# Column sums in four column strips, later q and k loads without a wait for V, and the first layer's first groups ahead of a unit's products with V

## The chip, the cores and the metric

The kernel runs on one core of one Trainium2 chip. The metric is the device time of one execution in microseconds (us), lower is better. Before the change it is 308.14 us, the median of three runs (307.33 to 308.79). The traces come from the hardware profiler and show one execution each.

## What is computed

Attention in a sliding window over 8 sequences of 576 tokens with 8 heads of 64, and then a two-layer block on the 4608 rows of 512 that come out of it:

```python
scores = scale * np.matmul(q, k.transpose(0, 1, 3, 2))
mask = np.abs(pos[:, None] - pos[None, :]) <= window      # window = 32
scores = np.where(mask, scores, -1000000000.0)
attn = np.exp(scores - np.max(scores, axis=-1, keepdims=True))
attn = attn / (np.sum(attn, axis=-1, keepdims=True) + 1e-09)
x = np.matmul(attn, v)                                    # as (4608, 512)
...
h = x @ w_in                                              # 512 x 2048
r = np.maximum(h, 0.0)
g = s * (r * r) + b
out = g @ w_out                                           # 2048 x 512
```

Since `g @ w_out` is `s * (r*r) @ w_out + b * (column sums of w_out)`, the kernel adds a row of column sums of w_out, times b, to each output row. That row is called CVEC.

## The kernel before

**Who sets the order.** Every operation is a task of one of five streams (TensorE "pe", ScalarE "act", VectorE "dve", GpSimd "pool", and "sp", which issues the DMAs), with what it reads and writes, a cost and a key. A planner (`_Graph.plan`) runs the tasks through a model of the engines and takes, again and again, the task that can start first; the key decides between tasks that could start at the same time. The result is one fixed order for each engine. Each engine then works through its order strictly, and a task that waits holds up all that stands behind it on its engine. All loads and stores, and the DMA transposes, go through the one queue of SP.

**Attention.** The tokens are worked in units of 128 (`unit`, `finish`): the scores of a unit (`qk_part`), exp on ScalarE, a mask on VectorE, the products with V (`av_part`, line 839), a reciprocal and a scaling on VectorE, and a transposition into XT, the input of the first layer. The V of a unit is loaded as f32 (line 589) and cast to bf16 into VB (lines 597 and 598); EV0, EV1 and EV2 name the engine of that cast for the first, the second and the later sequences. Units are counted through: sequence 0 has units 0 to 4 and so on; from sequence 3 on (LONG = 3) all tokens are one long row with units 0 to 22 in the trace's order, of which the last sequence begins at unit 18.

**q and k.** For the first three sequences they are cast, turned by TensorE (lines 628, 660, 673) and copied to SBUF. From sequence 3 on (`later`, `piece`) they are loaded in three pieces (lines 707 and 714: q, k, and the last 64 tokens of both), cast on ScalarE or POOL (line 733) and turned by DMA transposes (line 749). A piece waits for an earlier unit's products (`paced`), and, before the change, for the load of the last V unit of the sequence before it. Units from number 25 on are also turned into XT by DMA transposes (line 887).

**The first layer.** Blocks of 512 tokens; the first three blocks are cut smaller (SPLIT: block 0 into 224, 128 and 160 tokens, blocks 1 and 2 into two times 256). `s1` computes some columns of 128 of the hidden layer: matmuls on TensorE into one of two banks W (line 1097), ReLU on ScalarE (line 1104), the square on VectorE (line 1110). FIRST lists the order in which the first pieces (token piece, quarter of the 2048 columns) are made. W_in and W_out come in 8 loads each (line 561) and are cast by POOL (line 564).

**The second layer.** `second` makes each block of 512 tokens in seven products instead of eight (line 1154), with sums and differences of the hidden layer (line 1146) and of W_out (line 1126, `weight_sums`, partly in place in W_out). VectorE combines products into the output rows (line 1170), SP stores them (line 1179).

**The first minute of a run.** `first_units` makes the products with V of sequence 0: unit 2 and later wait for the transposition of the unit two before. `constant` makes CVEC: 16 matmuls with a weight matrix of ones add up the rows of W_out over 16 chunks of 128 rows, in one bank (line 1228), and VectorE multiplies by b (line 1231). Because the weights are all ones and 128 wide, each of the 128 output rows gets the same sums.

Of the kernel before, what the change touches and what calls it, by code (L numbers as in the profile page):

```python
# [5 lines left out]
F32 = mybir.dt.float32  # L6
# [3 lines left out]
ALU = mybir.AluOpType  # L10
# [11 lines left out]
PAIRS = 3  # L22
# [7 lines left out]
ORDER2 = ("t", "q0", "k0", "v0", "q1", "k1", "v1", "v2", "v3", "v4")  # L30
WINE = ("pool", "pool", "pool", "pool")
SPLIT = {0: (224, 128, 160), 1: (256, 256), 2: (256, 256)}
FIRST = ((0, 0), (1, 0), (0, 1), (2, 0), (1, 1), (2, 1), (0, 2), (1, 2), (2, 2), (0, 3), (1, 3), (2, 3))
WOUTE = (("pool", "pool"),) * 4
SWITCH = 215.0
XTS = 4000.0
# [4 lines left out]
PACE = ((-1, -1, -1),) * 3  # L41
CASTS = 40.0
LATE = 8
# [2 lines left out]
SLACK = (1000.0, 2000.0, 3000.0, 3000.0)  # L46
PACEV = ((-1,-1,0,0,1),(0,0,1,1,2),(0,0,1,1,2))
EARLY = -22.0
EV0 = ("dve", "act", "pool", "dve", "pool")
BANK1 = ("O", "AVN", "SC", "O", "AVN")  # L50
EV1 = ("pool", "pool", "pool", "pool", "pool")
EV2 = ("dve",) * 5
# [270 lines left out]
def bass_sliding_window_symmetric__then__act_starrelu_kernel(  # L323
# [23 lines left out]
    with ExitStack() as es:  # L347
        uid = {"n": 0}

        def seq_of(b):  # L350
            return min(b, LONG)
# [7 lines left out]
        def sb(shape, dt, nm):  # L359
            uid["n"] += 1  # L360
            return es.enter_context(nc.sbuf_tensor(f"{nm}_{uid['n']}", list(shape), dt))
# [39 lines left out]
        TW = [sb((128, 8, HN), BF16, "tw") for _ in range(3)]  # L401
        GSUM = sb((128, 8, HT), BF16, "gsum")
        CVEC = sb((128, DM), F32, "cvec")
        SB128 = sb((128, 2), F32, "sb128")
        SROW = sb((128, 2), F32, "srow")

# [14 lines left out]
        add = g.add  # L421
# [34 lines left out]
        def group_of(b):  # L456

            if b < LONG:
                return range(NUNIT)
            u0 = (NTILE * (b - LONG)) // 2  # L460
            return range(u0, (NTILE * (b + 1 - LONG) + (b == B - 1)) // 2)
# [106 lines left out]
        def paced(b, u):  # L568

            c, v = seq_of(b - 1), group_of(b - 1)[0] + u  # L570
            while v < 0:
                c, v = c - 1, v + NUNIT
            return land["av", c, v]
# [180 lines left out]
        def later(b, key):  # L754
            slot = b % 2
            if b < PAIRS + 2:
                for c0, x in ((0, 0), (160, WIN + S)):
                    add("pool", lambda e, c0=c0: e.memset(QTS[slot][:, :, c0:c0 + 16], 0.0), 400,
                        writes=[("QTZ", slot, x)] + [(t, slot, x, pr) for t in ("QT", "KT") for x in range(NTILE) for pr in range(NPAIR)],
                        key=key - 20.0)  # L760
            for i, parts in enumerate(((("q", 0, 512, 0),), (("k", 0, 512, 0),), (("q", 512, 64, 0), ("k", 512, 64, 64)))):
                piece(b, parts, key + 0.01 * i, [paced(b, PACE[min(b, 4) - 2][i])] +
                      ([land["v", seq_of(b - 1), group_of(b - 1)[-1]]] if b > PAIRS or LATE == PAIRS else []))

# [125 lines left out]
        def pe_part(key, av=None, sc=None, waits=()):  # L892

            parts = [p for p in (av, sc) if p]
            fns, mark = list(sc[0]) if sc else [], None
            if av:
                mark = len(av[0][0]) - 1
                fns = av[0][0] + fns + [None] + av[0][1]
            t = add("pe", fns, SWITCH + sum(p[3] for p in parts) + (0.0 if sc else 20.0),
                    reads=[r for p in parts for r in p[1]], writes=[r for p in parts for r in p[2]], key=key,  # L900
                    slack=1500.0 if key < due(2, 0) - 1 else SLACK[2], waits=waits)
            t.mark = mark
            return t
# [58 lines left out]
        def first_units():  # L962
            for u in range(NUNIT):
                bank, res = av_banks(0, u)
                stir(("av", u), res[0], bank[:, 0, :], -25.0 + u)
                land["av", 0, u] = pe_part(-25.0 + u, av=av_part(0, u), waits=[land["xt", u - 2]] if u > 1 else [])
                finish(0, u, -25.0 + u)

        last, closed = [], [0]
# [25 lines left out]
        def attention():  # L995
            seq = {"k": -200.0}

            def nxt():
                seq["k"] += 1.0
                return seq["k"]  # L1000

            def weights(step):
                which, i, x = {"w": "in", "o": "out"}[step[0]], int(step[1]), "ab".index(step[2])
                load_weights(which, i, x, nxt(), WINE[i] if which == "in" else WOUTE[i][x])

            for pr in range(NPAIR):
                for name in "qk":
                    load_pair(name, pr, nxt())
                    turn_pair(name, pr, -60.0 + 0.1 * pr, banks, K0[pr] if name == "k" else Q0[pr], 200.0)
                pair_scores(0, pr)  # L1010
            for t in ORDER0:
                if t == "t":
                    part(0, "t", nxt(), -23.5, banks, 200.0)
                    late_scores()
                elif t[0] == "v":
                    u = int(t[1])
                    load_v(0, u, nxt(), "sp")
                    cast_v(0, u, -28.0 + u, EV0[u], 300.0)
                else:
                    weights(t)  # L1020
            first_units()
            for step in ORDER1:
                if step == "s":
                    yield S
                elif step == "c":
                    for i, src in enumerate((moe_s, moe_b)):
                        add("sp", lambda e, i=i, src=src: e.dma_start(SROW[0:128:32, i:i + 1], src.partition_broadcast(4)),
                            600.0, writes=[("SROW", i)], dma=("l", 1, 15.0), key=nxt())
                    add("dve", lambda e: e.stream_shuffle(SB128[:, :], SROW[:, :], [0] * 32), 150,
                        reads=[("SROW", 0), ("SROW", 1)], writes=[("SB128", 0), ("SB128", 1)], key=P2[0, 0] - 8.0, slack=500.0)  # L1030
                elif step[0] in "wo":
                    weights(step)
                elif step[0] == "v":
                    load_v(1, int(step[1]), nxt(), "sp")
                    cast_v(1, int(step[1]), EARLY + 1.0 + 0.1 * int(step[1]), EV1[int(step[1])], 800.0)
                else:
                    part(1, step, nxt(), EARLY + 0.1 * FOURS.index(step), banks1, 500.0)
                    if step[0] == "k":
                        for pr in (2 * int(step[1]), 2 * int(step[1]) + 1):
                            pair_scores(1, pr)  # L1040
            pe_part(EARLY + 1.0, None, qk_part(1, NUNIT - 1))
            exp_mask(1, NUNIT - 1, EARLY + 1.0)
            for u in range(NUNIT):
                last.append((1, u))
                close()
            yield 2 * S
            for b in range(2, B):
                c = seq_of(b)
                if b >= PAIRS:
                    later(b, due(c, group_of(b)[0]) - 24.0)  # L1050
                else:
                    for step in ORDER2:
                        if step[0] == "v":
                            load_v(b, int(step[1]), nxt(), "sp")
                        else:
                            part(b, step, nxt(), due(b, 0) - 4.0 + 0.1 * FOURS.index(step), banks2, 1500.0)
                for i, u in enumerate(group_of(b)):
                    if b >= PAIRS:
                        load_v(c, u, due(c, u) - 35.0, late(b), [paced(b, PACEV[min(b, 4) - 2][i])])
                    cast_v(c, u, due(c, u) - 4.0, EV2[i], SLACK[3])  # L1060
                for u in group_of(b):
                    unit(c, u)
                    yield closed[0]
            if seq_tiles(LONG) % 2 == 0:
                unit(LONG, seq_units(LONG) - 1)
            while last:
                close()
            yield T
# [11 lines left out]
        def group(m):  # L1080
            return 4 if TBLK[m][1] <= 128 else 2 if TBLK[m][1] <= 256 else 1
# [141 lines left out]

        def constant():

            for i in range(8):
                f0 = 2 * i
                add("pe", [lambda e, fc=fc: e.matmul(SC[:, 0, :], lhsT=ONESW[:, :], rhs=WOUT_BF[:, fc, :],  # L1228
                                                     start=(fc == 0), stop=(fc == 15)) for fc in (f0, f0 + 1)],
                    440, reads=["ONESW", ("Wout", i // 2, i % 2)], writes=[("SC", 0)], accum=i > 0, key=P2[0, 0] - 4.0 + 0.1 * i)  # L1230
            add("dve", lambda e: e.tensor_scalar(CVEC[:, :], SC[:, 0, :], SB128[:, 1:2], None, ALU.mult),
                680, reads=[("SC", 0), ("SB128", 1)], writes=[("CVEC", x) for x in (0, 1)], key=P2[0, 0] - 2.0)

        units, made = attention(), 0

# [271 lines left out]
```

## Time and profile before

| What | Value |
|---|---|
| median of three runs | 308.14 us (307.33 to 308.79) |
| the profiled execution, in all | 308.89 us |
| its span in the trace | 307.2 us |
| its mean granted TensorE clock | 0.993 |
| moved by DMA | 54.30 MB, 177 GB/s on average |
| line 1228, 128x512 matmuls | 16, 379 ns each from start to end, between 49.5 and 57.6 us |
| DMA from issue to landing, median | V 4.8 us, q 1 MB 6.0 us, k 256 KB 6.5 us, XT transposes 3.3 us, stores 3.6 us |

The profile's page gives the busy time of each engine (PE is TensorE's matmuls, PEld its weight loads, DVE VectorE, ACT ScalarE, POOL GpSimd). A row of the view in order of time has the start, the length, the engine, the source line, what is written and read, the shape, how many instructions are merged in the row, and in brackets the idle time ahead of it and what ended it. A matmul's length goes from its start to its end, so that matmuls in a row overlap; the time that one costs is the distance to the next start. A row of the view by stages has the stage, its length, the busy time of PE, PEld, DVE, ACT and POOL with the number of instructions, the clock granted to TensorE (1.00 is full), the busy share of the DMA engines and GB/s. Line numbers are those of the kernel before.

### The profile page before, as it was taken

What the parts mean: (1) busy time and instruction counts of PE and PEld (TensorE: products, weight loads), DVE (VectorE), ACT (ScalarE), POOL (GpSimd) and SP (SyncE); (2) the same over time, 40 slices, a digit from 0 to 9 for tenths busy, and PEclk for the clock granted to TensorE, in tenths of its full rate; (3) what the DMA queues carried; (4) which work ended last, traced back from release to release, by engine and by line L of the source; (5) the groups of instructions that cost most, each with busy time, mean ns of one, the idle gap of its engine ahead of it and who ended that gap; (6) DMA issues with size and microseconds to landing.
All of it is one profiled execution on the core that took longest, in us unless ns stands there. A gap on an engine that the chain in (4) does not pass through costs nothing.

```text
span 307.2 us, 8786 instructions
## 1 busy us (share of the span) xinstructions
PE 294.9 (96%) x3837; PEld 213.4 (69%) x3837; DVE 233.2 (76%) x401; ACT 156.7 (51%) x244; POOL 66.4 (22%) x79
## 2 busy tenths in 40 slices
PE   8879899999999999999999999989999999999994
PEld 3458687798888887666766666656666666666783
DVE  3556788699879697989798768995877776566673
ACT  3746775685895564655554544542554433333200
POOL 5344587300000270055047000450000000000000
PEclk9979999999999999999999999999999999999999
DMA  7999999999994997999699679999513110210223
GB/s 204 290 246 302 325 291 370 268 227 273 159 232 125 239 202 160 279 201 178 184 255 198 132 172 273 186 201 150 153 21 88 53 47 31 74 34 2 69 70 107
DMA packets 120152, 54.30 MB, mean 177 GB/s; under 512 B 94816, under 2 KB 115936, under 8 KB 120112
## 3 DMA queue, kind: packets, MB, share of 16 engines
q1 hardware_dynamic: 120112, 53.72, 75.0%
q8 instruction: 31, 0.51, 0.8%
q14 instruction: 9, 0.07, 0.1%
HBM read 36.70 MB, written 9.44 MB: 150 GB/s over the span
## 4 chain that ended last, share of the span: by engine, by line
PE 79%; SPq 4%; DMA 3%; DVE 2%; issue 1%; POOL 0%
PE w L1097 36%; PE o L1154 31%; PE avn L839 4%; SPq L714 3%; DMA stg<-in_moe_w_in_dram 2%; PE sc L1154 2%; PE sc L781 2%; PE avn L870 1%; PE sc L1228 1%; DMA vst<-in_v_dram 1%; DVE outs L1170 1%; DVE gt L1110 1%; SPq L887 0%; SPq L707 0%; POOL win L564 0%
## 5 line engine op out<-in xcount | busy, mean ns | idle before, releaser
L1097 PE MATMUL w<-xt,win 128*128 128x512 bf16 (+4 forms) x832 | 145.7, 316 | 1.3 <-POOL win L564 1.3
L1104 ACT ACTIVATE r<-w 128x512 bf16<-128x512 f32 (+2 forms) x148 | 86.6, 586 | 105.6 <-PE w L1097 103.9
L1097 PEld LDWEIGHTS w<-xt,win 128*128 128x128 bf16 x832 | 75.6, 99 | 35.9 <-POOL win L564 1.9
L1110 DVE TENSOR_TENSOR gt<-r 128x1024 bf16<-128x1024 bf16 (+3 forms) x100 | 63.6, 639 | 24.9 <-ACT r L1104 24.2
L1154 PE MATMUL o<-wout,gt 128*128 128x256 bf16 x528 | 66.5, 273 | 0.0
L1154 PEld LDWEIGHTS o<-wout,gt 128*128 128x128 bf16 x528 | 50.8, 98 | 13.3
L733 POOL CAST nat<-stg 128x1024 bf16<-128x1024 f32 (+2 forms) x28 | 33.7, 1202 | 78.8 <-DMA stg<-in_q_dram 65.0
L809 ACT ACTIVATE ex<-sc 128x1024 bf16<-128x1024 f32 (+1 forms) x29 | 29.7, 1023 | 12.4 <-PE avn L839 10.8
L1154 PE MATMUL o<-tw,gt 128*128 128x256 bf16 x272 | 34.6, 273 | 0.0
L1154 PEld LDWEIGHTS o<-tw,gt 128*128 128x128 bf16 x272 | 26.2, 98 | 7.0
L1170 DVE SCALAR_TENSOR_TENSOR outs<-o,sb,cvec 128x512 f32<-128x512 f32 (+1 forms) x36 | 25.7, 715 | 4.3 <-PE o L1154 4.3
L1170 DVE SCALAR_TENSOR_TENSOR outs<-o,sb,outs 128x512 f32<-128x512 f32 (+1 forms) x27 | 19.3, 716 | 6.7 <-PE o L1154 6.6
L1146 DVE TENSOR_TENSOR gt<-gt 128x1024 bf16<-128x1024 bf16 (+1 forms) x26 | 23.8, 916 | 0.4
L813 DVE TENSOR_TENSOR ex<-ex,mask 128x1024 bf16<-128x1024 bf16 (+1 forms) x29 | 22.5, 775 | 0.6
L863 DVE TENSOR_TENSOR xn<-avn,rec 128x512 bf16<-128x512 f32 (+1 forms) x31 | 21.3, 687 | 0.7
L839 PE MATMUL avn<-vb,ex 64*64 64x65 bf16 x944 | 19.9, 197 | 1.9 <-issue 1.6
L839 PEld LDWEIGHTS avn<-vb,ex 64*64 64x64 bf16 x944 | 13.0, 106 | 11.5 <-issue 8.0
L598 DVE CAST vb<-vst 128x512 bf16<-128x512 f32 (+1 forms) x30 | 13.1, 444 | 9.5 <-DMA vst<-in_v_dram 9.5
L1154 PE MATMUL o<-tw,gsum 128*128 128x256 bf16 x136 | 17.7, 273 | 0.0
L1154 PEld LDWEIGHTS o<-tw,gsum 128*128 128x128 bf16 x136 | 12.8, 98 | 3.3
L1146 DVE TENSOR_TENSOR gsum<-gt 128x1024 bf16<-128x1024 bf16 x18 | 13.2, 731 | 0.3
L878 ACT COPY xt<-avn 128x512 bf16<-128x512 bf16 (+2 forms) x19 | 10.0, 533 | 4.8 <-PE avn L870 4.8
(119 smaller groups left out, 225.4 us busy)
## 6 DMA issues: line engine op xcount, KB each, us to landing
vst<-in_v_dram SPq DMA_DIRECT2D x32, 256.0 KB, 4.8
out_dram<-outs SPq DMA_DIRECT2D x32, 256.0 KB, 3.6
stg<-in_k_dram SPq DMA_DIRECT2D x24, 256.0 KB, 6.5
stg<-in_q_dram SPq DMA_DIRECT2D x5, 1024.0 KB, 6.0
stg<-in_moe_w_in_dram SPq DMA_DIRECT2D x8, 512.0 KB, 7.4
stg<-in_moe_w_out_dram SPq DMA_DIRECT2D x8, 512.0 KB, 7.4
stg<-in_q_dram SPq DMA_DIRECT2D x4, 512.0 KB, 8.2
stg<-in_k_dram SPq DMA_DIRECT2D x4, 512.0 KB, 8.4
```

What stands on the lines that cost most here:

```text
L598: (lambda e: e.tensor_copy(VB[0:n, vb, :, 0:D], VST[0:n, vs, :, :])),
L733: (lambda e, dst=dst, src=src: e.tensor_copy(dst, src)),
L809: add("act", lambda e, dst=flat_dst, src=flat_src: e.activation(dst, src, AF.Exp, bias=0.0, scale=0.125), 190 + 0.833 * 512 * len(hs), rea ...
L813: add("dve", lambda e, flat=flat, mask=mask: e.tensor_tensor(flat, flat, mask, ALU.mult), 130 + 0.53 * 512 * len(hs), reads=[("E", ei, hp, ...
L839: return [lambda e: e.matmul(av[64 * x:64 * x + 64, h, 0:D + 1], lhsT=buf[64 * g:64 * g + 64, h % 2, h // 2, c:c + 64], rhs=VB[64 * g:64 * ...
L863: add("dve", lambda e: e.tensor_tensor(XN[xi][0:p1, :].rearrange("p (a c) -> p a c", a=H), av[0:p1, :, 0:D], REC[ri][0:p1, :].rearrange("p ...
L1097: add("pe", [lambda e, g=g, kc=kc: e.matmul(wt[:, g, :], lhsT=WIN_BF[:, kc, (f0 + g) * 128:(f0 + g + 1) * 128], rhs=XT[:, kc, t0 % XR:t0 % ...
L1104: add("act", lambda e: e.activation(rt, wt, AF.Relu, bias=0.0, scale=1.0), 190 + 0.833 * ng * nt, reads=[("W", wb)], writes=[("R1", rb, ha ...
L1110: add("dve", lambda e: e.tensor_tensor(GT[gs][:, f1:f1 + nf, g0:g0 + nt], rr, rr, ALU.mult), 130 + 0.55 * nf * nt, reads=[("R1", rb, x) fo ...
L1146: add("dve", lambda e: e.tensor_tensor(dst, x, y, op), 1240.0 if half is None else 690.0, reads=reads, writes=writes, key=k)
L1154: add("pe", [lambda e, g=g, j=j, dst=dst: e.matmul(dst, lhsT=lhs[:, g, 128 * j:128 * j + 128], rhs=rhs[:, g, :], start=first and g == 0 an ...
L1170: add("dve", lambda e, src=src, dst=dst, other=other: e.scalar_tensor_tensor(dst, src, SB128[:, 0:1], other, ALU.mult, ALU.add), 200 + 1.0 ...
```

## The change

Five edits:

- **Column sums.** Each of four groups now has four matmuls with only 32 of the columns of ones. Their outputs go to the four strips of 32 partitions of the bank, and each strip adds up four of the 16 chunks. ScalarE copies the bank to SBUF, and one f32 matmul with a matrix PART of 1/32 adds up the four strips and spreads the sums over all 128 rows. PART is filled on VectorE.
- **The first groups of the first layer.** `first_units` makes the first two groups on token piece 0 ahead of the products of unit 2, and these wait for them; the entry (0, 0) goes from FIRST.
- **EV0.** The V cast of unit 1 moves from ScalarE to POOL.
- **Later loads.** A piece of q and k no longer waits for V of the sequence before.
- **Their key.** The key of `later` is 8 earlier.

```diff
-FIRST = ((0, 0), (1, 0), (0, 1), (2, 0), (1, 1), (2, 1), (0, 2), (1, 2), (2, 2), (0, 3), (1, 3), (2, 3))
+FIRST = ((1, 0), (0, 1), (2, 0), (1, 1), (2, 1), (0, 2), (1, 2), (2, 2), (0, 3), (1, 3), (2, 3))
...
-EV0 = ("dve", "act", "pool", "dve", "pool")
+EV0 = ("dve", "pool", "pool", "dve", "pool")
...
+        PART = sb((128, 128), F32, "part")
...
-                piece(b, parts, key + 0.01 * i, [paced(b, PACE[min(b, 4) - 2][i])] +
-                      ([land["v", seq_of(b - 1), group_of(b - 1)[-1]]] if b > PAIRS or LATE == PAIRS else []))
+                piece(b, parts, key + 0.01 * i, [paced(b, PACE[min(b, 4) - 2][i])])
...
-                land["av", 0, u] = pe_part(-25.0 + u, av=av_part(0, u), waits=[land["xt", u - 2]] if u > 1 else [])
+                if u == 2:
+                    for ft in range(0, 4, group(0)):
+                        s1(0, ft)
+                    ahead = [t for t in g.tasks if t.stream == "pe"][-1]
+                land["av", 0, u] = pe_part(-25.0 + u, av=av_part(0, u), waits=[land["xt", u - 2]] + [ahead] if u > 1 else [])
...
-                    later(b, due(c, group_of(b)[0]) - 24.0)
+                    later(b, due(c, group_of(b)[0]) - 32.0)
...
-            for i in range(8):
-                f0 = 2 * i
-                add("pe", [lambda e, fc=fc: e.matmul(SC[:, 0, :], lhsT=ONESW[:, :], rhs=WOUT_BF[:, fc, :],
-                                                     start=(fc == 0), stop=(fc == 15)) for fc in (f0, f0 + 1)],
-                    440, reads=["ONESW", ("Wout", i // 2, i % 2)], writes=[("SC", 0)], accum=i > 0, key=P2[0, 0] - 4.0 + 0.1 * i)
-            add("dve", lambda e: e.tensor_scalar(CVEC[:, :], SC[:, 0, :], SB128[:, 1:2], None, ALU.mult),
-                680, reads=[("SC", 0), ("SB128", 1)], writes=[("CVEC", x) for x in (0, 1)], key=P2[0, 0] - 2.0)
+            key = P2[0, 0] - 4.0
+            add("dve", lambda e: e.memset(PART[:, :], 1.0 / 32), 150, writes=["PART"], key=-20)
+            for r in range(4):
+                add("pe", [lambda e, r=r, c=c: e.matmul(SC[32 * c:32 * c + 32, 0, :], lhsT=ONESW[:, 0:32], rhs=WOUT_BF[:, 4 * r + c, :],
+                                                        start=(r == 0), stop=(r == 3), skip_group_check=True) for c in range(4)],
+                    300.0, reads=["ONESW"] + [("Wout", r, x) for x in (0, 1)], writes=[("SC", 0)], accum=r > 0, key=key + 0.1 * r)
+            add("act", lambda e: e.copy(CVEC[:, :], SC[:, 0, :]), 617.0, reads=[("SC", 0)], writes=[("CVEC", x) for x in (0, 1)], key=key + 0.5)
+            add("pe", lambda e: e.matmul(SC[:, 1, :], lhsT=PART[:, :], rhs=CVEC[:, :], start=True, stop=True), 1000.0,
+                reads=["PART"] + [("CVEC", x) for x in (0, 1)], writes=[("SC", 1)], key=key + 0.6)
+            add("dve", lambda e: e.tensor_scalar(CVEC[:, :], SC[:, 1, :], SB128[:, 1:2], None, ALU.mult),
+                680, reads=[("SC", 1), ("SB128", 1)], writes=[("CVEC", x) for x in (0, 1)], key=P2[0, 0] - 2.0)
```

Because the planner works with the new tasks and waits, the order of TensorE, ScalarE and VectorE also changes elsewhere, mostly between 20 and 180 us. In the built order of SP, all loads up to the third sequence stand as before; the q and k loads of the last sequence move ahead of two transpositions into XT, two loads of V and three stores.

## The prediction

> **What bounds the kernel now.** I read the page's engine shares first, then the busy time by stage, then TensorE's waits, then instructions in order of time where a wait or an idle piece stood. The page says that TensorE is the engine to watch:
>
> ```profile
> PE 294.9 (96%) x3837; PEld 213.4 (69%) x3837; DVE 233.2 (76%) x401; ACT 156.7 (51%) x244; POOL 66.4 (22%) x79
> ```
>
> The stages say where the missing 12 us lie (length; busy PE, PEld, DVE, ACT, POOL; granted clock; DMA):
>
> ```profile
> 16.00:19.40 3.40, 1.50 (x44) 0.95 (x32) 0.90 (x2) 2.79 (x6) 1.66 (x2) 1.00 1.03 235
> 19.40:22.80 3.40, 3.30 (x46) 2.65 (x47) 2.76 (x5) 0.66 (x2) 1.04 (x1) 0.50 0.90 243
> ...
> 200.00:220.00 20.00, 18.38 (x236) 12.29 (x226) 14.97 (x26) 8.90 (x13) 4.13 (x4) 1.00 1.02 171
> ```
>
> A 3.4 us stretch with 1.50 us of TensorE work is followed by 3.4 us at clock 0.50. The other hole is one of 1.62 us near 207; from 61 to 206 TensorE waits for nothing. In order of time, the start:
>
> ```profile
> 19.43 0.94 PE L839 MATMUL sc<-vb,ex 64*64 64x65 bf16 x32 [1.43 <-POOL vb L598]
> 20.30 2.90 PE L1097 MATMUL w<-xt,win 128*128 128x224 bf16 x16
> 25.37 1.04 POOL L564 CAST win<-stg 128x1024 bf16<-128x1024 f32 x1 [1.87 <-DMA stg<-in_moe_w_in_dram]
> 26.47 0.94 PE L1097 MATMUL w<-xt,win 128*128 128x224 bf16 x8 [0.21 <-POOL win L564]
> 36.63 0.94 PE L1097 MATMUL w<-xt,win 128*128 128x224 bf16 x8 [1.05 <-POOL win L564]
> ```
>
> Weights come as DMA brings them, POOL casts them at once, and TensorE waits for the casts. The same at the end of the loading:
>
> ```profile
> 56.28 1.04 POOL L564 CAST wout<-stg 128x1024 bf16<-128x1024 f32 x1 [0.77 <-DMA stg<-in_moe_w_out_dram]
> 57.35 2.36 DVE L1126 TENSOR_TENSOR tw<-wout 128x2048 bf16<-128x2048 bf16 x2 [1.44 <-POOL wout L564]
> 57.38 0.60 PE L1228 MATMUL sc<-wout,onesw 128*128 128x512 bf16 x2
> 60.29 1.22 DVE L1126 TENSOR_TENSOR wout<-wout,tw 128x2048 bf16<-128x2048 bf16 x1
> 61.56 0.61 PE L1154 MATMUL o<-wout,gt 128*128 128x256 bf16 x4
> ```
>
> The last W_out cast ends at 57.32. The last pair of column sums starts at 57.38, the differences of W_out at 57.35, the in-place difference ends at 61.51, and the second layer's first product starts at 61.56. This is a gate: it is tied to a DMA landing, not to TensorE's earlier work. And the hole:
>
> ```profile
> 185.50 0.47 SPq L707 DMA_DIRECT2D stg<-in_q_dram  x1
> 186.00 8.29 SPq L714 DMA_DIRECT2D stg<-in_k_dram  x4
> 203.29 2.49 SPq L749 DMA_TRANSPOSE kt<-nat  x1
> 208.09 0.32 PE L839 MATMUL avn<-vb,ex 64*64 64x65 bf16 x16 [1.62 <-issue]
> ```
>
> The task at 208.09 holds the last sequence's first scores. It needs the turned k, issued at 203.29, from loads that went out only at 185.50.
>
> **The change part by part.** 1. *V of unit 1 cast on POOL.* POOL is idle from 13.71 to 15.26; such a cast takes 0.61 there. TensorE's wait for ScalarE's cast was 0.46. What follows is set by the copies into XT (ScalarE, unit 1's ends at 18.20), so I count nothing; without the POOL gap it would cost up to 0.6.
>
> 2. *First two groups ahead of unit 2's products.* They need W_in's second cast (17.91) and XT of unit 1 (18.20): start 18.2. Eight such matmuls take 0.77 to the next start at full clock (26.47), so 16 end at 19.75 and unit 2's products at 20.4; before, both were done at 22.95. That is 2.5 us ahead. But the built order of the changed program then has unit 3's products, unit 2's transposes, unit 4's products and next the group of columns 512 to 1023 on block 0, which needs the cast that ends at 26.41. Behind it wait unit 3's transposes (0.22), the mask matmuls (0.44) and block 1's first quarter (16 matmuls, 0.90), which before ran at 24.5 to 26.2. So at 26.45 TensorE is behind by 1.56. And from 22.8 to 26.2 it has 0.39 + 0.69 = 1.1 us of work, less than the 1.50 that went ahead of the clock drop. I take half clock from 26.2 to 29.6: (29.6 - 26.45) / 2 = 1.57 more. Bounds for that: 0 (clock stays) and 1.7 (a whole window). Before waited 0.35 + 1.05 between 34 and 36.6, which takes up 1.4. At 38.7: 1.56 + 1.57 - 1.40 = **1.7 late**.
>
> 3. *Column sums.* Before: 16 matmuls of 128x512, 0.2175 each (the pair at 57.38 to 57.82): 3.48. After: four groups of four with 32 columns of weights. In the trace the 64x64 score products run four at a time (16 of 128 columns in 0.41, 0.22 of it latency, so 0.2 against 0.85 one by one), with two column halves on the same rows. So I take a group as one matmul, 0.22, plus two changes of tile size at 0.1 (the eight transposes from 32.34 are through by 32.78, the 64x64 products behind them start at 32.88): 0.4; bounds 0.3 and 1.1 (one after another). Up to the gate: 14 x 0.2175 = 3.05 go, 3 x 0.4 come, and one first-layer task of 0.87 now also stands ahead: 1.0 less. So TensorE comes to the gate 1.7 - 1.0 = 0.7 late. Behind it stood 0.44 + 1.75 + 0.22 + 1.75, now 0.4 + 1.75 + f32 product + 0.22 + 0.87. For the f32 product no row exists. Below: a bf16 one, 0.22; above: the 16 it stands in for, 3.5. Both its operands have twice the bytes, so I take 4 x 0.2175 = 0.9. It waits for ScalarE's copy (0.62), which 1.75 of matmuls cover; uncovered it would cost up to 0.8. The path from the gate is then 4.14 against 4.16, and the first product starts **0.6 late** (the chain of DVE would let it start at 61.4 at the earliest, so no more than 0.15 can be won up to here). DVE is full from 60 to 70 (10.0 of 10), its copy of k sets the scores near 71, and 0.1 of the lateness goes there: **+0.5**.
>
> [...]
>
> 4. *Later loads.* Without the wait for V and with an earlier key, the last sequence's seven loads stand right behind V of unit 16 (176.71), so they start at 177.2, not 185.5. They hold SP for about 10.2. Past them are moved: XT of units 11 and 12, V of units 17 and 18, three stores. V 17 goes out at 188.7 and lands 5.5 later, at 194.2; its products are at 205.4. A store moves from 183.64 to 191.2 and lands 3.6 later (194.8); its buffer is written again at 196.64. XT of unit 14 now goes behind the four turns: issue 203.2, landing 3.3 later, 206.5; block 6 wants it at 207.9, as one score task and two products were ordered ahead. The turns of q and k start near 194.2; from the first turn to TensorE it took 8.3 (199.82 to 208.09), so 202.5 against a need at 205.4. The hole goes: **-1.65**. The earlier sequences' loads move by little, and there TensorE had no wait.
>
> Sum: 307.2 + 0.5 - 1.65 = 306.05 for the span, 1.15 less. That execution took 308.89 in all against a median of 308.14, so I take the difference to the median: **307.0**.
>
> **The rivals.** *B, the start costs nothing:* the clock stays, or drops elsewhere, and some of the sums' saving survives. [...] Against: the gate. Between -0.15 and -1.0 with -1.65: 305.5 to 306.3, say 305.9.
>
> *C, the wait moves (slower):* SP's burst of 10.2 us makes XT of unit 14 late. It decides from a landing after 207.9; each us later costs one, and from 209 on the kernel is slower than before. The margin is 1.4; turns here take 1.22 to 4.44 to issue, and an XT turn at 179.88 took 3.72. With a landing at 211: 3.1 in place of 1.65, with 0.5: 310.1. The same place also delays stores and V.
>
> *D, the loads do no good:* the turned k is bound by casts and DMA traffic, the hole stays: 308.14 + 0.5 = 308.6. Against: POOL idles 24.5 us for that q.
>
> *E, the four strips run one by one:* three groups ahead of the gate take 0.87 + 0.2 each, 2.0 more; the fourth 0.65 more. 307.0 + 2.65 = 309.7. Against it are the score products, four at a time. [...]
>
> **How the numbers follow.** Forecast 0.38, B 0.28, C 0.16, D 0.12, E 0.06. 0.5% is 1.5 us, about what a measurement of this kernel tells from no change: faster is below 306.6, slower above 309.7. Faster: 0.26 of B and 0.11 of the forecast (its f32 bound, a clock that drops for less): 0.37. Slower: 0.13 of C, 0.04 of E, 0.02 of D: 0.19. Same: 0.44. The range reaches down through B and up to where C begins in earnest, 305.3 to 309.6; the forecast's own is 306.2 to 307.9.
>
> **What would show it.** The granted clock at 19.4 to 22.8 should be full and half near 26 to 30; the group on the cast of 26.4 should wait about 2 us; the four strips should start within 20 ns of each other; the second layer's first product should start between 61.4 and 62.3; no wait at the last sequence's scores, and none at block 6's first group. The forecast is wrong if TensorE stands more than 0.5 us anywhere from 62 to 210, or if the first product starts before 61.

## The result and the profile after

The changed kernel takes 311.94 us, the median of five runs (309.79 to 312.79), against 308.14 for the kernel before (307.33 to 308.79, five runs): 1.0114 times as long, with a 95% interval of 1.0086 to 1.0142. Run again beside other runs of the kernel before it took 312.61 (six runs), 1.014 times as long (1.0101 to 1.0178). The forecast was 307.0, with 305.3 to 309.6 as its range: the change loses some 4 us where 1.15 were to be won.

The profiled execution is the fastest of its five, 309.79 in all and 308.1 in the span, 0.9 more than before. It shows less than the median loses, so a second trace is read beside it below. Line numbers of the changed kernel are up to 8 higher than before (1097 is now 1101, 1154 is 1158). Some matmul records are missing (3809 against 3839 weight loads); idle pieces of 0.16 marked "issue" are these.

```profile
PE 292.0 (95%) x3809; PEld 212.5 (69%) x3839; DVE 231.8 (75%) x402; ACT 156.4 (51%) x244; POOL 66.4 (22%) x80
```

**The start.** In order of time, the first two groups on TensorE, the transposition of unit 2, unit 4's products and the group on columns 512 to 1023; below it the stages, cut at the change of clock:

```profile
18.69 1.69 PE L1101 MATMUL w<-xt,win 128*128 128x224 bf16 x16 [0.28 <-POOL win L565]
22.25 0.40 PE L870 MATMUL sc<-ident,xn 128*128 128x128 bf16 x4 [0.66 <-DVE xn L863]
23.21 0.77 PE L839 MATMUL avn<-vb,ex 64*64 64x65 bf16 x24 [0.57 <-POOL vb L599]
24.66 1.67 PE L1101 MATMUL w<-xt,win 128*128 128x224 bf16 x8 [0.68 <-POOL win L565]
```

```profile
16.87:20.28 3.41, 2.63 (x41) 2.01 (x38) 1.16 (x3) 3.28 (x7) 1.65 (x2) 1.00 1.08 268
20.28:23.70 3.42, 1.95 (x91) 1.29 (x92) 2.67 (x8) 1.27 (x3) 1.81 (x3) 1.00 1.09 251
23.70:27.12 3.42, 2.52 (x25) 2.02 (x27) 1.06 (x3) 0.75 (x2) 1.51 (x2) 0.50 1.10 325
```

In this trace the two groups run at full clock, 1.69 against 2.90 before. But the work that used to fill the waits is now gone from them: TensorE stands for 1.9 us in three waits between 21.6 and 24.7, is busy for 1.95 of 3.42, and the next 3.42 run at half clock.

**The gate at W_out.** In order of time: the last cast of W_out, the differences on VectorE, and TensorE with the last strips, the f32 product and the second layer's first product:

```profile
55.94 1.20 POOL L565 CAST wout<-stg 128x1024 bf16<-128x1024 f32 x1 [1.25 <-DMA stg<-in_moe_w_out_dram]
...
57.34 2.35 DVE L1130 TENSOR_TENSOR tw<-wout 128x2048 bf16<-128x2048 bf16 x2
59.95 1.21 DVE L1130 TENSOR_TENSOR wout<-wout,tw 128x2048 bf16<-128x2048 bf16 x1
...
55.41 0.40 PE L1233 MATMUL sc<-wout,onesw 128*32 128x512 bf16 x4
55.75 1.92 PE L1101 MATMUL w<-xt,win 128*128 128x256 bf16 x16
57.60 0.40 PE L1233 MATMUL sc<-wout,onesw 128*32 128x512 bf16 x4
...
59.69 1.02 PE L1237 MATMUL sc<-cvec,part 128*128 128x512 f32 x2
60.55 0.39 PE L661 MATMUL avn<-ident,nat 128*128 128x128 bf16 x4
```

From one start to the next, four strips take 0.34 (55.41 to 55.75) and the f32 product 0.86 (59.69 to 60.55). The last cast ends at 57.14 (57.32 before), and the first product starts at 61.64 (61.56 before). Whatever the start and the sums may save ends at this gate.

**The middle, where the kernel before had no wait.** TensorE at the transpositions of the last units of blocks 3 and 4, with ScalarE's copy behind the second, then VectorE and POOL ahead of the first:

```profile
118.42 0.40 PE L870 MATMUL avn<-ident,xn 128*128 128x128 bf16 x4 [0.57 <-DVE xn L863]
119.72 0.59 PE L1101 MATMUL w<-xt,win 128*128 128x512 bf16 x2 [0.90 <-ACT xt L878]
...
144.13 0.40 PE L870 MATMUL avn<-ident,xn 128*128 128x128 bf16 x4 [0.83 <-DVE xn L863]
144.36 1.03 PE L1101 MATMUL w<-xt,win 128*128 128x512 bf16 x4
...
144.56 0.58 ACT L878 COPY xt<-avn 128x512 bf16<-128x512 bf16 x1 [1.50 <-PE avn L870]
```

```profile
115.33 1.41 DVE L1150 TENSOR_TENSOR gsum<-gt 128x1024 bf16<-128x1024 bf16 x1
116.66 0.20 DVE L861 RECIPROCAL rec<-avn 128x8 f32<-128x8 f32 x1
116.78 0.98 DVE L1150 TENSOR_TENSOR gt<-gt 128x1024 bf16<-128x1024 bf16 x1
117.68 0.68 DVE L863 TENSOR_TENSOR xn<-avn,rec 128x512 bf16<-128x512 f32 x1
...
111.53 5.68 POOL L734 CAST nat<-stg 128x1024 bf16<-128x1024 f32 x5 [3.88 <-DMA stg<-in_k_dram]
```

The same place in the kernel before, on TensorE, and one of its sums of the hidden layer with POOL idle:

```profile
115.86 0.39 PE L870 MATMUL avn<-ident,xn 128*128 128x128 bf16 x4
116.08 1.91 PE L1154 MATMUL o<-wout,gt 128*128 128x256 bf16 x16
117.83 1.89 PE L1097 MATMUL w<-xt,win 128*128 128x512 bf16 x8
...
117.97 0.69 DVE L1146 TENSOR_TENSOR gsum<-gt 128x1024 bf16<-128x1024 bf16 x1
```

The planner worked with other times in the start and came to another order up to block 5. The transposition of the last unit that block 3 needs now stands right ahead of that block's first group, so TensorE waits for the scaling (0.57) and then for the copy into XT (0.90); before, two products (16 matmuls) stood between them. At block 4's last unit TensorE waits for the scaling alone (0.83): the group behind that transposition starts at 144.36, before the copy into XT does at 144.56, so it does not need this unit. There one group and one product stand between the unit's products with V and its transposition, where two groups and a product stood before. On VectorE the sums of the hidden layer go ahead of the scaling, and beside POOL's casts they are slow: 1.41 here for a sum that takes 0.69 when POOL is idle. These three waits cost 2.3. The hole at the last sequence's first scores is gone, which gives 1.62 back. 0.1 + 2.3 - 1.6 = 0.8 of the 0.9.

### The profile page after: what moved, and what is told of

It is laid out like the page before. It is cut to its first block, busy times and chain, and to the rows that moved or that the text cites. A ratio compares the mean times of both kernels' runs of the same rounds, so it can differ in the third digit from the quotient of the medians.

```text
span 308.1 us, 8772 instructions
## 1 busy us (share of the span) xinstructions
PE 292.0 (95%) x3809; PEld 212.5 (69%) x3839; DVE 231.8 (75%) x402; ACT 156.4 (51%) x244; POOL 66.4 (22%) x80
## 4 chain that ended last, share of the span: by engine, by line
PE 87%; DVE 6%; DMA 2%; issue 2%; ACT 1%; SPq 0%; POOL 0%
PE w L1101 39%; PE o L1158 32%; PE avn L839 4%; PE sc L781 2%; PE sc L1158 2%; DMA stg<-in_moe_w_in_dram 2%; DVE gt L1114 2%; PE w L615 2%; PE avn L870 1%; DVE gsum L1150 1%; DVE xn L863 1%; ACT r L1108 1%; DVE kt L653 1%; PE w L629 1%; DVE outs L1174 1%
## 5 line engine op out<-in xcount | busy, mean ns | idle before, releaser
L1101 PE MATMUL w<-xt,win 128*128 128x512 bf16 (+4 forms) x805 | 139.0, 313 | 4.6 <-issue 1.6
L1101 PEld LDWEIGHTS w<-xt,win 128*128 128x128 bf16 x832 | 74.4, 98 | 35.7 <-ACT xt L878 1.3
L1114 DVE TENSOR_TENSOR gt<-r 128x1024 bf16<-128x1024 bf16 (+3 forms) x100 | 62.6, 635 | 34.4 <-ACT r L1108 34.1
L809 ACT ACTIVATE ex<-sc 128x1024 bf16<-128x1024 f32 (+1 forms) x29 | 29.7, 1023 | 12.8 <-PE avn L839 11.5
L813 DVE TENSOR_TENSOR ex<-ex,mask 128x1024 bf16<-128x1024 bf16 (+1 forms) x29 | 20.9, 719 | 1.1
L839 PEld LDWEIGHTS avn<-vb,ex 64*64 64x64 bf16 x944 | 12.9, 107 | 10.2 <-issue 6.2
L1150 DVE TENSOR_TENSOR gsum<-gt 128x1024 bf16<-128x1024 bf16 x18 | 14.1, 784 | 0.3
```

The lines of the kernel that those rows point to most:

```text
L809: add("act", lambda e, dst=flat_dst, src=flat_src: e.activation(dst, src, AF.Exp, bias=0.0, scale=0.125), 190 + 0.833 * 512 * len(hs), rea ...
L813: add("dve", lambda e, flat=flat, mask=mask: e.tensor_tensor(flat, flat, mask, ALU.mult), 130 + 0.53 * 512 * len(hs), reads=[("E", ei, hp, ...
L839: return [lambda e: e.matmul(av[64 * x:64 * x + 64, h, 0:D + 1], lhsT=buf[64 * g:64 * g + 64, h % 2, h // 2, c:c + 64], rhs=VB[64 * g:64 * ...
L1101: add("pe", [lambda e, g=g, kc=kc: e.matmul(wt[:, g, :], lhsT=WIN_BF[:, kc, (f0 + g) * 128:(f0 + g + 1) * 128], rhs=XT[:, kc, t0 % XR:t0 % ...
L1114: add("dve", lambda e: e.tensor_tensor(GT[gs][:, f1:f1 + nf, g0:g0 + nt], rr, rr, ALU.mult), 130 + 0.55 * nf * nt, reads=[("R1", rb, x) fo ...
L1150: add("dve", lambda e: e.tensor_tensor(dst, x, y, op), 1240.0 if half is None else 690.0, reads=reads, writes=writes, key=k)
```

## The experiments

Each is compared with the kernel before on the same chip. Where only hunks of the change are made, they are named by the lines that they add. Two explanations are followed through: theory S puts the loss into the start, by stretches at half clock, and theory M into the middle, by the new waits near 118 and 144.

**1. The changed kernel once more**

> The changed kernel once more, to see a run with the lower mean clock (0.987 to 0.989 in four of its five runs; 0.993 in the one whose trace is at hand). Theory S (start): the median is again near 311.9, and a profile with a clock near 0.988 shows two stretches of about 3.4 us at half clock between 15 and 45 us, against one in the trace at hand, and the rest of the span as there; the second stretch costs 1.7 to 2. Theory M (middle): the waits at 118 (0.57 + 0.90) and 144 (0.83) are in every run, and the lost 2 us of the slower runs stand there too, as a clock drop behind the 1.5 us of idle TensorE near 118 (stage 120 to 124 below 1.00). If the profiled run has 0.993 again, this stays open.

312.61 us, 1.014 (1.0101 to 1.0178). The profiled run has a span of 309.5 and a clock of 0.981. Stages, cut at the changes of clock, and the gate:

```profile
14.46:17.87 3.41, 2.29 (x69) 1.53 (x68) 1.80 (x4) 1.18 (x4) 1.29 (x3) 1.00 1.14 251
17.87:21.29 3.42, 2.65 (x29) 2.00 (x28) 1.29 (x3) 2.70 (x6) 1.65 (x2) 0.50 0.99 246
21.29:24.70 3.41, 2.81 (x73) 1.91 (x72) 1.63 (x7) 0.86 (x2) 1.88 (x3) 0.50 1.07 248
24.70:28.12 3.42, 3.35 (x41) 2.58 (x41) 1.54 (x3) 1.01 (x2) 1.62 (x2) 0.50 1.11 327
```

```profile
55.90 1.27 POOL L565 CAST wout<-stg 128x1024 bf16<-128x1024 f32 x1 [0.51 <-DMA stg<-in_moe_w_out_dram]
...
58.93 0.40 PE L1233 MATMUL sc<-wout,onesw 128*32 128x512 bf16 x4
...
62.97 1.04 PE L1158 MATMUL o<-wout,gt 128*128 128x256 bf16 x8
```

Not one stretch at half clock but three in a row, 10.25 us. TensorE comes to the last strips 1.76 after the last cast (58.93 against 57.17; in the other trace 0.46), and the first product is 1.3 later than there. So the gate hides what the start saves, but not what it loses. The waits of the middle are here too (0.46, 0.68 and 1.10). The clock does not sort the runs by itself, though: the changed kernel's eleven runs have 0.981 to 0.993 and 309.8 to 314.1, the kernel before has 0.982 to 0.994 in 23 runs and 307.0 to 309.9.

**2. The first groups without the rest**

```diff
+                if u == 2:
+                    for ft in range(0, 4, group(0)):
+                        s1(0, ft)
...
+EV0 = ("dve", "pool", "pool", "dve", "pool")
```

The first run makes both hunks, the second leaves V of unit 1 on ScalarE.

> The first two groups ahead of unit 2's products and V of unit 1 on POOL, without sums and later loads. Theory S: nothing won at the gate of W_out near 61.5, the hole at 207 stays, and a second stretch at half clock in the start in most runs: about 308.1 + 0 to 2, clock near 0.988. Theory M: the first group of block 3 stands two tasks behind its transposition (no wait there), that of block 4 right behind it (0.8): 308.1 + 0.8 = 308.9. Rival (the first groups win what they win at the start): 307 or less.

> The first two groups ahead of unit 2's products alone, V of unit 1 still cast on ScalarE. Theory S: the same loss as with V on POOL: 311.5 to 312.5. Rival (the cast of V on POOL is what sets the start back, by the casts of k and W_in behind it): 309 to 310.

With V on POOL 312.10, 1.010 (1.0062 to 1.0138); with V on ScalarE 311.76, 1.0077 (1.0042 to 1.0112). The first groups alone bring most of the loss, and the engine of that cast matters little. The two traces have 6.8 and 13.7 us at half clock. In the first, TensorE reaches the last column sums 3.6 after the last cast; POOL and TensorE in order of time:

```profile
54.88 1.19 POOL L564 CAST wout<-stg 128x1024 bf16<-128x1024 f32 x1 [0.61 <-DMA stg<-in_moe_w_out_dram]
...
59.70 0.59 PE L1232 MATMUL sc<-wout,onesw 128*128 128x512 bf16 x2
...
211.72 0.32 PE L839 MATMUL avn<-vb,ex 64*64 64x65 bf16 x16 [1.96 <-DMA kt<-nat]
```

The last row is the hole at the last sequence's first scores: 1.96 here, and there is none in the second trace, though neither kernel changes the loads.

**3. Later loads alone, later loads with the sums, and the kernel before again**

```diff
-                      ([land["v", seq_of(b - 1), group_of(b - 1)[-1]]] if b > PAIRS or LATE == PAIRS else []))
...
+                    later(b, due(c, group_of(b)[0]) - 32.0)
```

> Before with the later loads alone (no wait for V, key 8 earlier). Its built order on TensorE is that of before up to the third block of 512, so theories S and M both expect the hole of 1.62 us near 207 gone and nothing in its place: 308.1 - 1.65 = 306.5, ratio 0.9945 to 0.9955. Rival L (the loads are what costs: SP's burst or POOL's casts, which lengthen VectorE's work beside them, delay the middle): 308.1 or more, with a new wait of TensorE between 100 and 205.

> Later loads and the sums in four groups, without the first groups ahead and with V of unit 1 cast on ScalarE. In the built order the first group of block 3 stands two products behind its transposition, as before, and that of block 4 right behind it, as in the changed kernel. Theory M: no wait at 118, one of 0.8 to 1.0 near 144; with the start as before 308.1 - 1.65 + 0.8 = 307.3. Theory S: 306.5, since the start has its one stretch at half clock at 19.4 as before. Rival (the sums are the loss): 309 or more.

> The kernel before once more, for a second trace of the last sequence's first scores. If the hole of 1.62 us near 207 is in every run, it is 1.3 to 2.0 here, and the later loads took it away and lost the gain elsewhere; if it belongs to one run, it is below 0.5, and the later loads had nothing to win in most runs.

Loads alone: 308.60, 0.9996 (0.9967 to 1.0025). Loads and sums: 308.24, 0.9993 (0.9972 to 1.0013). Neither wins what the hole was to give. The second trace of the kernel before shows a reason, in order of time at the last sequence's first scores:

```profile
207.81 0.32 PE L839 MATMUL avn<-vb,ex 64*64 64x65 bf16 x16 [0.34 <-DVE gsum L1146]
```

Here the hole has 0.34 in place of 1.62 (a third trace with this order, in experiment 6, has 0.30). With the two traces of experiment 2, five traces with the old loads have 1.62, 0.34, 0.30, 1.96 and nothing: the size of that hole changes from one execution to the next. And with the loads alone block 6's first group waits for the transposition of unit 14 into XT, which SP issues behind the four turns at 204.68 and which lands at 207.58 (the row names an exp on ScalarE, but that ended at 206.72):

```profile
207.67 0.59 PE L1096 MATMUL w<-xt,win 128*128 128x512 bf16 x2 [1.04 <-ACT ex L808]
...
204.68 1.22 SPq L886 DMA_TRANSPOSE xt<-xn  x1
```

With sums and loads the wait at block 4's last unit is the one that theory M expected, and larger; TensorE, VectorE and POOL:

```profile
141.52 0.40 PE L870 MATMUL avn<-ident,xn 128*128 128x128 bf16 x4 [1.51 <-DVE xn L863]
...
135.57 1.52 DVE L1146 TENSOR_TENSOR gsum<-gt 128x1024 bf16<-128x1024 bf16 x1
137.12 1.41 DVE L1146 TENSOR_TENSOR gt<-gt 128x1024 bf16<-128x1024 bf16 x1
138.45 1.52 DVE L1110 TENSOR_TENSOR gt<-r 128x1024 bf16<-128x1024 bf16 x1
139.89 0.74 DVE L1170 SCALAR_TENSOR_TENSOR outs<-o,sb,outs 128x512 f32<-128x512 f32 x1
140.55 0.19 DVE L861 RECIPROCAL rec<-avn 128x8 f32<-128x8 f32 x1
...
134.06 6.38 POOL L734 CAST nat<-stg 128x1024 bf16<-128x1024 f32 x5 [2.69 <-DMA stg<-in_k_dram]
```

The unit's products with V are done at 138.2, but its reciprocal comes at 140.55, behind a difference and a square that take twice their 0.69 beside POOL's casts (1.41, 1.52) and an output row. The sums save nothing at the gate: from the end of the last cast to the first product it is 4.66 with them and 4.41 with the loads alone.

**4. The middle: five tasks moved in the finished order**

```diff
+        g.order = ahead_of(g.order, [(scaled[number(LONG, 2)], 1), (turned[number(LONG, 2)], 1), (scaled[number(LONG, 6)], 2)])
```

`scaled` holds a unit's reciprocal and scaling (two tasks; the text below says four tasks, with the transposition they are five), `turned` its transposition; `ahead_of` moves them so many places ahead on their engine and keeps everything else.

> The changed kernel with four tasks moved in the finished order and nothing else: on VectorE the reciprocal and the scaling of the last unit that block 3 needs go one place ahead (in front of the sums of the hidden layer), those of block 4's last unit two places (in front of a square and an output row), and on TensorE the transposition of block 3's last unit goes in front of the product of 8 that stood before it. Theory M: the waits of 0.46 to 0.57 and 0.7 to 0.9 near 119 and of 0.8 to 1.1 near 145 go, less what the moved work then delays: 312.3 - 2 = 310.3, ratio to before 1.006; the start is as bad as in the changed kernel (first product of the second layer between 61.6 and 64). Rival (the wait only moves on, since VectorE is what is behind): 312, with a new wait within 10 us.

310.69, 1.0065 (1.0033 to 1.0096): 1.9 less than the changed kernel in experiment 1. TensorE at block 3:

```profile
120.81 0.39 PE L873 MATMUL avn<-ident,xn 128*128 128x128 bf16 x4
121.03 1.04 PE L1162 MATMUL o<-wout,gt 128*128 128x256 bf16 x8
122.12 1.67 PE L1105 MATMUL w<-xt,win 128*128 128x512 bf16 x7
```

No wait, and none at block 4. From the first product to TensorE's end it takes 240.5, against 242.4 and 242.6 in the two traces of the changed kernel: the 1.9 is won there. This trace begins with four stretches at half clock (18.5 to 32.1) and has its first product only at 65.64 (2.5 of that because the last cast of W_out ends at 59.71), and neither wait of the middle is there all the same: the two losses are separate.

**5. The start: TensorE's idle places filled**

```diff
+        for n, deps, ahead in ((2, [], land["turn", 1]), (2, [], land["late"][0]), (3, land["late"][1:], land["turn", 2]),
+                               (3, land["late"][1:], land["av", 0, 4])):
+            dummies(n, deps, ahead)
```

`dummies` puts n matmuls of ones, 128x512, into a bank that is free at that point, in front of the named task.

> The changed kernel with ten matmuls of 128x512 without use put into TensorE's idle places of the start: two in front of the transposition of unit 1, two in front of the late scores, three in front of the transposition of unit 2 and three in front of unit 4's products; all else in the same order. They take 10 x 0.2175 = 2.2 us at full clock, about as much as TensorE waits there (2.2 in the trace of the changed kernel). Theory S (the start loses by half clock): at most one stretch at half clock between 15 and 30, mean clock 0.993 or more, the first product of the second layer back at 61.5 to 62, 1.4 earlier than in the second trace of the changed kernel: 312.3 - 1.4 = 310.9. Rival (the start loses by its chains on VectorE and ScalarE, the clock is only a sign of it): clock better, time 312 or, with the dummies in the way, 313.

310.77, 1.008 (1.0041 to 1.0119). The mean clock of its twelve runs is 0.9962, against 0.9858 in the six of experiment 1. Stages, and TensorE at the gate:

```profile
18.02:21.40 3.38, 3.38 (x31) 2.10 (x30) 0.80 (x2) 2.44 (x5) 1.66 (x2) 0.51 0.87 228
21.40:24.80 3.40, 2.91 (x80) 1.81 (x78) 3.26 (x8) 1.23 (x3) 1.95 (x3) 0.99 1.08 265
```

```profile
57.20 0.40 PE L1236 MATMUL sc<-wout,onesw 128*32 128x512 bf16 x4
...
61.25 0.93 PE L1161 MATMUL o<-wout,gt 128*128 128x256 bf16 x7
```

One stretch at half clock, TensorE in time for the last strips (0.23 after the cast ends at 56.97), and the first product 1.7 earlier than in experiment 1, by 2.2 us of matmuls that compute nothing. This speaks for theory S, in which the clock is a loss and not only a sign of one. The medians alone do not settle it: 310.77 is 1.8 below experiment 1, but the intervals of the two ratios overlap (1.0041 to 1.0119, 1.0101 to 1.0178), and four of the twelve runs take over 312 with clocks of 0.992 to 0.997.

**6. Both cures, and versions without the first groups**

The moved tasks and the dummies in the changed kernel; then sums and loads on the old start with block 4's two tasks moved, without and with ten dummies; and the kernel before with these dummies:

```diff
+        for n, deps, ahead, bank in ((2, [], land["turn", 1], AVN), (2, [], land["late"][0], AVN),
+                                     (6, land["copies"], land["av", 0, 2], W)):
+            dummies(n, deps, ahead, bank)
```

> The changed kernel with both cures: ten matmuls without use in the start, and the four tasks of blocks 3 and 4 moved ahead. If theories S and M are both right and independent, the first product is at 61.3 and the rest takes the 240.6 us that it took with the moved tasks: 301.9 for TensorE's end, some 307.5 in all, ratio 0.995 to 0.998: the changed kernel is then no slower than before. Rival (one loss hides the other): 309 to 311.

> Sums in four groups and later loads, without the first groups and with V of unit 1 on ScalarE, and the reciprocal and the scaling of block 4's last unit two places ahead on VectorE. Theory M: the wait of 1.51 at 141.5 goes: 308.2 - 1.5 = 306.7, ratio 0.994 to 0.996. Rival (it moves on): 308.2.

> Sums in four groups and later loads on the old start (no first groups, V of unit 1 on ScalarE), block 4's reciprocal and scaling two places ahead, and ten matmuls without use in the start: two in front of the transposition of unit 1, two in front of the late scores, six in front of unit 2's products. From the first product of the second layer to the end the same order without the dummies took 238.5 us, and a start that comes to the gate in time has that product at 61.3: 299.8 for TensorE's end, some 305.4 in all, ratio 0.989 to 0.992. Rival (the start's half clock is hidden by the gate anyway): 308, as without the dummies.

> The kernel before with the ten matmuls without use in its start, in front of the transposition of unit 1, the late scores and unit 2's products; all other orders the same. If the gate at W_out hides what the start loses in the kernel before, the clock rises to 0.995 and the time stays within 0.5 of 308.5. If the stretches at half clock cost it something too, 307 to 308.

| Kernel | us | Ratio to before (95%) |
|---|---|---|
| changed, both cures | 309.46 | 1.0019 (0.9990 to 1.0048) |
| sums and loads, tasks moved | 308.12 | 0.9970 (0.9939 to 1.0001) |
| the same with dummies | 307.22 | 0.9971 (0.9936 to 1.0005) |
| before with dummies | 307.68 | 0.9985 (0.9961 to 1.0009) |

With both cures the changed kernel can't be told from the kernel before. But beside kernels that have the same help it is still slower: 309.46 against 307.22 for sums and loads on the old start with dummies and 307.68 for the kernel before with dummies, all on one chip and all with a mean clock of 0.998. So 1.8 to 2.2 us that come with the first groups are neither the half clock nor the waits of the middle (resampling the runs gives 95% intervals of 0.7 to 2.3 and 1.0 to 2.9). No version is clearly faster than the kernel before; the best median is 1.4 below it, with 1 inside the interval. The first three medians lie 1.4 to 2 above what was expected of them. In the trace of the first, all from the first product on takes 240.2, as expected, but the last cast of W_out ends only at 59.56, and TensorE waits for it:

```profile
59.61 0.40 PE L1240 MATMUL sc<-wout,onesw 128*32 128x512 bf16 x4 [1.64 <-POOL wout L565]
```

Over the fourteen traces that cast ends between 56.07 and 59.71; past 58 it is in three of seven with the first groups and in one of seven without. Three of these four have 10 to 14 us at half clock, this one none. What moves it stays open. In all four late traces SP's issue of W_in's third load ends only at 18.07 to 18.71, in the other ten at 16.10 to 17.96; it began at 14.2 to 14.7, before the first groups, which speaks against these as the cause of the late cast. In the kernel before, the dummies raise the clock to 0.993 to 1.000; 307.68 lies where it was expected if the half clock costs that kernel something too, but the interval holds 1, so this stays open. On the old start the gate hides most of it.

The traces put together (H: us at half clock; G to O: from the end of the last W_out cast to the first product's start; O to E: from there to TensorE's end; where a cell has several numbers, one for each trace):

| Kernels | H | G to O | O to E |
|---|---|---|---|
| before, two traces | 3.4, 6.8 | 4.24, 4.61 | 241.5, 241.1 |
| old start, loads; with sums; with moved tasks | 3.4, 6.8, 10.2 | 4.41, 4.66, 4.8 | 241.0, 240.2, 238.5 |
| the last of these with dummies; before with dummies | 0, 0 | 4.5, 4.2 | 239.3, 240.3 |
| changed, two traces | 3.4, 10.2 | 4.50, 5.80 | 242.4, 242.6 |
| first groups with V on POOL, on ScalarE | 6.8, 13.7 | 7.8, 5.5 | 242.8, 241.7 |
| changed, moved tasks | 13.7 | 5.9 | 240.5 |
| changed, dummies; both | 3.4, 0 | 4.3, 4.1 | 243.0, 240.2 |

On the old start G to O stays between 4.2 and 4.8 with 10 us at half clock as with none. On the new start it is 4.1 to 4.5 with up to 3.4 us at half clock, and 5.5 to 7.8 with 6.8 or more.

O to E less TensorE's waits in it (those above 0.2) falls into three groups, and these go by how many matmuls of the first layer TensorE has run when the first product starts: 240.8 to 240.9 with 256 of them (first groups alone), 239.9 to 240.3 with 264 (the kernel before, the loads alone, and the changed kernel in all versions), 238.5 to 238.9 with 272 (sums and loads on the old start). Eight of these take 0.87. So on the old start the time that the sums save at the gate is used for one more group ahead of it, and the changed kernel has one group less there. That is 0.9 of the 2.2 us above; against the kernel before with dummies, which has 264 as well, it explains nothing.

## Why the prediction was wrong

**Where it was right.** V of unit 1 on POOL costs nothing that can be measured (312.10 against 311.76). In the trace at hand the first groups run at full clock, the stretch at half clock moves behind them, and the group on W_in's fourth cast waits (0.68; about 2 was forecast). That is in part luck of that execution: in three other traces with the first groups (experiment 1, the moved tasks, V on ScalarE) the half clock begins between 17.9 and 18.9, and they run in it: 3.15 with the moved tasks and 3.14 with V on ScalarE instead of 1.69. A group of four strips costs 0.34 (forecast 0.4) and the f32 product 0.86 (0.9, the author's estimate from the bytes of its operands, which no row of before shows), so rival E is out. The gate at W_out takes all that the sums save. The turned k no longer holds the last sequence.

**The step that failed** stands at the end of part 4: "The earlier sequences' loads move by little, and there TensorE had no wait." From this the stretch from 62 to the last sequence was counted at nothing. The order there is not kept; the planner makes it new from whatever the start looks like. The new one has the transposition of block 3's last unit right ahead of the group that needs it, and that of block 4's last unit one group nearer to the products with V that it waits for, with VectorE's scaling in between. That cost 2.3 in one trace and 2.2 in the other, and 1.9 came back when five tasks were moved. The forecast's own sign of being wrong, a wait of more than 0.5 between 62 and 210, came three times (0.57, 0.90, 0.83). The diff does not name this place, but the built order of TensorE shows it before any run. The expectations in experiments 2 and 3 look for the second wait at block 4's first group, right behind a transposition; that transposition is of a later unit, which the group does not need, and the wait is one unit earlier.

**Two terms were mis-sized.** The clock drop was counted as one stretch, 1.57 for its half, and +0.5 at the gate. The trace at hand has one, and there the first product is 0.08 late. Another has three, with 1.4 late, and the first groups alone had two and four. The forecast's bound for it, "1.7 (a whole window)", was too near: in eleven cases here a stretch at half clock, with 2.10 to 2.82 us busy of its 3.41, is followed by another. (The forecast's own terms, 0.7 + 4.14 - 4.16, make the first product 0.7 late where it writes 0.6; that matters little.)

One program has its half clock at another point in each trace: in the changed kernel it begins at 23.71 and lasts 3.4 in one, and begins at 17.87 and lasts 10.2 in the other; in the kernel before it is 19.39 with 3.4, and 17.74 with 6.8. Over the traces it lasts 3.4, 6.8, 10.2 or 13.7.

The hole was counted at 1.65 from one execution; two others with the same order have 0.34 and 0.30, and of the two with the first groups alone one has 1.96 and one none. And part of what was left came back as rival C described it, at its place: XT of unit 14 behind SP's burst, 1.04 with the loads alone and 0.47 in the version with sums, moved tasks and dummies. In the changed kernel TensorE gets there 2.7 later (the unit before it starts at 187.74 against 185.04), and no such wait is seen.

**The sum again.** In the second trace of the changed kernel against the second of the kernel before: G to O 5.80 - 4.61 = 1.2, and O to E 242.6 - 241.1 = 1.5, so 2.7 of the 4 between the medians. The moved tasks took 1.9 of it away and the filled start 1.8, each in its own runs, the second not clear of the noise; both together some 3. That the middle's waits cost 1.9 is shown by moving them away. That the half clock delays the gate rests on the traces (5.5 to 7.8 against 4.1 to 4.5) and on one such cure. What is left beside kernels with the same cures has no shown cause; the changing end of W_out's loads may be in it.

The middle's slow VectorE was the cause of the waits' size, and it is the same in the kernel before, where something stood in front: a difference of the hidden layer takes 1.52 there at 111.59, while POOL casts (108.91 to 114.76), and 0.69 at 118.69, when POOL is idle. In the rows of the changed kernel and of experiment 3 the sums, differences and squares that run while POOL casts take 1.41 to 1.52.

## What to carry to other kernels

In a kernel whose order a planner makes, an edit at the start is an edit everywhere: read the built order of the bound engine from end to end for consumers that have come closer behind their producers, above all where the producer's engine is slow beside another (here a sum took 1.41 in place of 0.69 while POOL cast). Look at what the moved work leaves behind: here the first groups gained their own time in one trace (1.69 against 2.90), the two traces of the changed kernel have one and three stretches of 3.4 us at half clock against one and two in those of the kernel before, and matmuls put into the waits raised the mean clock from 0.9858 to 0.9962. A hole seen in one execution is an estimate with a spread: look at a second trace before counting on it. And a cure that helps is to be tried on the kernel before too, or it is credited with too much.

## What the runs showed of the hardware

- The clock changes at multiples of 3.41 us from its other changes: in the kernel before at 19.39, 22.81 and 306.11 (283.3 = 83 x 3.413), in the changed kernel at 23.71, 27.12 and 307.01 (279.9 = 82 x 3.413). In eight traces (both kernels, two of each, and experiments 2 with V on ScalarE, 4, 5 and 6 with moved tasks on the old start) it fell after full-clock stretches with 1.49 to 2.31 us of TensorE work. But busy time does not decide it alone: full-clock stretches with 1.75 (the filled start, at 140.9, with a wait of 1.54) and 1.93 (both cures, at 24.7, with a wait of 1.43) kept the clock. At half clock, eleven stretches with 2.10 to 2.82 us busy were followed by another at half, and seven with 3.18 or more by full clock; one with 2.52 recorded, in the first trace of the changed kernel, was followed by full clock too.
- Four matmuls of 128x512 in four strips of 32 columns take 0.34 from start to the next start (55.41 to 55.75), against 4 x 0.2175 = 0.87 for four of the kernel before, one after another.
- The f32 matmul of 128x512 takes 0.86 (59.69 to 60.55), 3.95 times the 0.2175 of its bf16 kind, and is recorded as two.
